# An expert-mixing and convolution kernel: the first matmuls, the first stage of the token transform, and the planner's price of a 16-bit transfer are changed

## The chip, the cores and the metric

The kernel runs on one core of one Trainium2 chip. The metric is the device time of one execution in microseconds (us). The kernel before took 1466.44 us, the median of three runs (1465.94, 1466.44 and 1466.64).

## What is computed

The input `x` has 2048 tokens of width 576. Two branches are computed from it and mixed by a gate for each token:

```python
g = _sigmoid((x * gate_w).sum(-1, keepdims=True))
a = _A_ref(x, ...)          # long convolution of each channel, plus x * Dskip
b = _B_ref(x, ...)          # 32 heads, each picks 2 of 4096 experts
return g * a + (1 - g) * b
```

Branch A builds a convolution kernel of 2048 taps for each of the 576 channels from 128 complex exponentials, and convolves through a discrete Fourier transform (`Kf`, `Uf`, `Yf = Uf * Kf`, inverse). Branch B makes queries `q = x w_q`, scores them against two tables of 64 keys, takes the best two of each, and from their sums the best two of the four pairs. Each chosen expert `e` contributes `g * gelu(x . u[e]) * v[e]`.

The kernel computes B densely. It has the score tiles (`x` times the product of `w_q` and the keys, then top two), the activation tiles (`x` times all 4096 rows of `u`), one-hot matrices that spread the gates over the experts, and at the end a product of the weighted activations with all 4096 rows of `v`. Values that need more than 16 bits are split into a high and a low half (`hi`, `lo`), both fp16, and three products are added: hi times hi, hi times lo and lo times hi.

## The kernel before

**The planner.** The Python program decides the order on each engine while it is built. `clock[0]` is the planner's time, and it goes forward with TensorE's (PE's) matmuls. Work beside the main loop is written as generators that `spawn` puts in a heap. A generator that has to wait yields, and `pump` resumes it when the planner believes that its operands are ready. `Engine` (lines 117 to 134) prices VectorE (DVE), ScalarE (ACT) and GpSimd (POOL) work; `dma` (199 to 204) prices a transfer at four bytes an element over 340 GB/s plus 2.2 us. The chip then runs each engine's list in that order; an instruction whose operands are late holds up all behind it on its engine.

**Main loop** (1563 to 1601). It hands PE either a score tile (`s`, a pair of eighth `c` of the heads and token block `t`, 128 in all) or an activation tile (`a`, a triple `c, tb, j`, 128 in all). Both are 14 matmuls with 512 moving columns (`triple`, 850 to 862). A score tile leaves work for DVE (`scores_top`), an activation tile one scaling copy on ACT or DVE and a store (`act_post`). A score tile needs `whl[c]`, which `w_half`, `w_fold` and `w_tail` make from two halves of `w_q`, and a quarter of the tokens, `xb[tb]`. An activation tile needs `uhl[c]` (from `u_build`) and `xb[tb]` (from `x_build`).

**The start.** SyncE issues in order the keys `kt`, the first quarter of the tokens (`xs`, `xr`), both halves of the first `w_q` (1152 KB each), then the first eighth of `u` (1024 KB and twice 128 KB) and the constants `cst`. `x_build(0)` squares the tokens, adds the squares over the partitions with five matmuls against ones, reduces to the largest norm on DVE (`nx`), turns it into a power of two (`root_scale`, four small DVE instructions), and splits. The first matmuls of the main loop are score tiles. Every tile waits for whole operands.

**Slots and banks.** Nine large buffers (`slot`) are shared by what is loaded and what is split. Eight PSUM banks are shared: four (`sc`) for the tiles, four (`kb`) for all else while the taps are made, after that `wb`.

**Branch A.** `k_params`, `k_front` and `k_gen` make the taps on POOL, ACT and DVE; `k_store` writes them to memory in fp16. `u_stage1` (977 to 1025) is the first stage of the tokens' transform: 32 positions, two interleaved generators (`half(0)`, `half(1)`). A position's tokens are loaded twice, into partitions 0 to 63 and 64 to 127; ACT makes `h` of all 128, DVE replaces the upper 64 by the low half, and for each half of the channels PE multiplies `h` by the tables `tu[:, 0]` and `tu[:, 1]` with 128 rows. It uses one bank at a time. When all taps are stored and `u_stage1` has ended, `freq` (1164 to 1200) runs beside the score tiles. It loads the taps again (`ksb`, four transfers of 1152 KB, each held back until the planner sees the wire free), then the tables `tk` (two of 1024 KB), runs `k_stage1`, then `products`, and afterwards opens the buffers for the one-hot matrices (`ab`) and spawns `prep(0)`.

**The end.** After the last tile the program waits until the activations are stored and `ab` exists (line 1602). The last loop (1611 to 1641) multiplies each block's weights, made by `prep`, with `v` (`o`), with the inverse transform (`y`) beside it.

Of the kernel before, what the change touches and what calls it, by code (L numbers as in the profile page):

```python
# [24 lines left out]
D = 576  # L25
# [19 lines left out]
def _tables():  # L45
# [24 lines left out]
    tu = np.ascontiguousarray(stacked(U_PAIRS).reshape(128, 32, 2, 128))  # L70
# [67 lines left out]
def body(ctx: ExitStack, tc: tile.TileContext, xT, au, par, logdt, dskip, gatew, wq, kT, uT, vv,  # L138
# [60 lines left out]
    def dma(o, i, q=None):  # L199
        t = max(clock[0], rdy.get(key(i), 0.0), queue[0])  # L200
        queue[0] = t + 0.45
        wire[0] = max(wire[0], t) + 4 * o.shape[0] * size(o) / 3.4e5
        rdy[key(o)] = max(rdy.get(key(o), 0.0), wire[0] + 2.2)
        (q or DQ).dma_start(o, i)
# [217 lines left out]

    def x_load(tb):
        a = slot([4, 512], F32, f"xs{tb}")
        r = pl.tile([128, 512], F32, tag="xr", name=f"xr{tb}", bufs=2)
        c = slice(512 * tb, 512 * tb + 512)
        dma(a, xT[0:512, c].rearrange("(k p) n -> p k n", p=128))
        dma(r[0:64], xT[512:576, c])
        dma(r[64:128], xT[512:576, c])
        return a, r  # L430
# [14 lines left out]

    def x_build(tb):
        while tb and tb - 1 not in scaled:
            yield 0.3
        if tb:
            yield from need("slot", 2)  # L450
            xl[tb] = x_load(tb)
        a, r = xl.pop(tb)
        while tb and 0 not in uhl:
            yield 0.3
        b = slot([9, 512], F16, f"xb{tb}")
        sq = b[:, 0:5].bitcast(BF16)
        yield from ready(a, r)
        if tb:
            S.activation(sq[:, 0:4, :], a, AF.Square)
        else:  # L460
            S.activation(sq[:, 0:2, :], a[:, 0:2], AF.Square)
            V.tensor_mul(sq[:, 2:4, :], a[:, 2:4], a[:, 2:4])
        S.activation(sq[:, 4, :], r, AF.Square)
        yield from ready(b)
        yield from need("kb")
        p = bank("kb", f"x{tb}")
        for k in range(5):
            mm(p, onesb, sq[:, k, :], k == 0, k == 4)
        yield from ready(p)
        V.tensor_reduce(out=nx[:, tb:tb + 1], in_=p, axis=AX, op=OP.max)  # L470
        free("kb", nx)
        s, i = root_scale(nx[:, tb:tb + 1], 1.02)
        V.tensor_copy(i_x[:, tb:tb + 1], i)
        yield from ready(s)
        for o, i in [(b[:, k], a[:, k, :]) for k in range(4)] + [(b[:, 8], r)]:
            if tb == 0 or S.free > V.free + 2.0:
                V.tensor_scalar(o, i, s, None, op0=OP.mult)
            else:
                S.activation(o, i, AF.Copy, scale=s)
        scaled.append(tb)  # L480
        for k in range(4):
            yield from ready(b)
            V.scalar_tensor_tensor(b[:, 4 + k], a[:, k, :], s, b[:, k], op0=OP.mult, op1=OP.subtract)
# [9 lines left out]
    whl, wl, sk, halves, scaled, squared = {}, {}, [], {}, [], []  # L493
# [23 lines left out]

    def w_half(c, h, w):
        fl = lambda x: x.rearrange("p a b -> p (a b)")
        yield from ready(w)  # L520
        pbs = []
        acc = newcol(True), newcol(True)
# [3 lines left out]
        squared.append(h)  # L526
        if c == 0:
            yield from w_fold(c, h, w, pbs, ("kb", "kb", "kb") if h == 0 else ("kb", "sc", "sc"))
# [3 lines left out]
        tag = side() if c else "sc"  # L532
# [12 lines left out]
        if c:  # L545
            yield from w_fold(c, h, w, pbs, (side(),) * 3)
        for k, tag, pb in pbs:
            spawn(w_tail(c, k, pb, hl, rem, o, count, s, tag), 0.3 * k)
        del pb, pbs
        free("slot")  # L550
        if c > 0:
            free("raw")
        if h == 0 and c > 0:
            spawn(w_next(c, 1))
# [25 lines left out]

    def w_next(c, h):
        while sdone[0] < c - (kdone[0] == NCK) and 8 * NT - len(groups) < NT * c - 5:
            yield 0.3
        yield from need("raw")
        take("raw", "raw")
        yield from need("slot")
# [304 lines left out]
    gated, placed = [], []  # L891
# [85 lines left out]
    def u_stage1():  # L977
# [5 lines left out]
        ended = []  # L983

        def half(m):
            for n in range(m, 2 * NT, 2):
                a, o = us[:, m, :], us[:, 2 + m, :]
                for z in range(2):
                    l, far = U_PAIRS[n]
                    dma(a[64 * z:64 * z + 64], bass.AP(tensor=au.tensor, offset=au.offset + l * D,  # L990
                                                       ap=[[64 * D, R1], [(far - l) * D, 2], [1, D]]))
                tu = uf.tile([128, 2, 128], F16, tag="tu", name=f"tu{n}", bufs=2)
                dma(tu, tu_d[:, n])
                yield from ready(a, tu)
                h = uf.tile([128, D], F16, tag="uh", name=f"uh{n}", bufs=2)
                S.activation(h, a, AF.Copy, scale=s_u)
                yield from ready(h)
                V.scalar_tensor_tensor(h[64:128], a[64:128], s_u[64:128], h[64:128], op0=OP.mult, op1=OP.subtract)
                yield from ready(h)
                for hh in range(2):  # L1000
                    tag = side()
                    yield from need(tag)
                    pb = bank(tag, f"u1_{n}_{hh}")
                    for z in range(2):
                        mm(pb[:, :288], tu[:, z], h[:, 288 * hh:288 * hh + 288], z == 0, z == 1)
# [4 lines left out]
                    del pb  # L1010
                yield from ready(ov)
                dma(pair_rows(su_d, n), o)
            ended.append(m)

        spawn(half(0))
        spawn(half(1), 3)
        while len(ended) < 2:
# [9 lines left out]
    def k_stage1(ksb, fk):  # L1027
# [11 lines left out]
        def load(w0):  # L1039
            tkt = fk.tile([128, 16, 2, 128], F16, tag="tk", name=f"tk{w0}", bufs=2)  # L1040
            dma(tkt, tk_d[:, w0:w0 + 16, :])
            return tkt

        tabs = load(0), load(16)
# [18 lines left out]
    def products(ff):  # L1063
# [21 lines left out]
        def tail(g, pbs, v):  # L1085

            t = ff.tile([128, 2, 2, PW], F32, tag="tt", name=f"tt{g}", bufs=2)
# [76 lines left out]
    def freq():  # L1164
# [4 lines left out]
        ksb = KS.__enter__().tile([128, 4, NCK // 2, 32, 2 * NI], F16, name="ksb")  # L1169
        for j in range(4):  # L1170
# [4 lines left out]
        fk = FK.__enter__()  # L1175
        spawn(v_norm(), 40)
        spawn(gating(0), 20)
        yield from k_stage1(ksb, fk)
# [21 lines left out]
        v_pool(5, 8)  # L1200


    def u_load(c):
# [3 lines left out]
        dma(a, uT[0:512, cs].rearrange("(k p) n -> p k n", p=128))  # L1207
        dma(r[0:64], uT[512:576, cs])
        dma(r[64:128], uT[512:576, cs])
        return a, r  # L1210

    uhl, i_u, uraw = {}, {}, []

    def u_build(c):
        while adone[0] < c - (kdone[0] < NCK or sdone[0] >= 7):
            yield 0.3
        yield from need("raw")
        take("raw", "raw")
        yield from need("slot")
        a, r = u_load(c)  # L1220
        uraw.append(c)
        yield from ready(a, r)
        while len(squared) < 2:
            yield 0.3
# [3 lines left out]
        yield from squares(a, r, sq, nu[:, c:c + 1])  # L1228
        s, i = root_scale(nu[:, c:c + 1], 1.02)
# [4 lines left out]
        rem = wrems[c % 2]  # L1234
        for k in range(4):
            yield from split(hl[:, 0, k, :], hl[:, 1, k, :], a[:, k, :], s)
        S.activation(rem[:, 0, :], r, AF.Copy, scale=s)
        yield from ready(rem)
        V.scalar_tensor_tensor(rem[0:64, 1, :], r[0:64], s[0:64], rem[0:64, 0, :], op0=OP.mult, op1=OP.subtract)
        free("slot", hl)  # L1240
        free("raw", hl)
        uhl[c] = hl, rem
        yield from ready(rem)
        if c < 7:
# [251 lines left out]
    def finish(t, po):  # L1496
# [7 lines left out]
        for d, o in au_rows(out, t, a):  # L1504
# [6 lines left out]
            for j in range(4)]  # L1511
    dma(kt, kT)
    xl = {0: x_load(0)}
    w_load(0, 0)
    w_load(0, 1)
    V.memset(onesb, 1.0)
# [7 lines left out]
    def k_split():  # L1524
# [159 lines left out]
```

## Time and profile before

| What | us |
|---|---|
| median of three runs | 1466.44 |
| the profiled execution | 1466.58 |
| its span, first to last instruction | 1464.7 |
| outside the span | 1.88 |
| last tap matmul (`kb`) starts | 606.5 |
| last product of the inverse (`pv`) starts | 936.4 |
| first matmul of the last loop (`o`) | 1009.14 |

The span is what the profile's rows add up to. A stage's busy share doesn't show how dense PE runs, since a matmul's row is longer than the time until the next can start; the distance of the rows of a run of matmuls shows it.

### The profile page before, as it was taken

Reading aid. Unit: us, or ns where it says so; the run is one execution under the profiler, and the core shown is the slowest. Engines: PE = TensorE matmul, PEld = TensorE weight load, DVE = VectorE, ACT = ScalarE, POOL = GpSimd, SP = SyncE. Lnnn points to the kernel's source line nnn. Section 1 sums busy time; section 2 is a strip of 40 time slices with the busy share of each in tenths; the row PEclk is TensorE's granted clock in tenths of the full one; section 3 lists DMA queues with packets and bytes.
Section 4 is the critical chain, followed back from the end, with each engine's and each line's share of the span. In section 5 each row is a group of like instructions: output and inputs, shape, how many; then the busy total and the mean of one; then the engine's idle time right before and its main releaser. Section 6 shows DMA issues by size and latency. Waiting matters only on the chain.

```text
span 1464.7 us, 36789 instructions
## 1 busy us (share of the span) xinstructions
PE 1431.2 (98%) x14025; PEld 858.4 (59%) x14028; DVE 1248.5 (85%) x4589; ACT 790.6 (54%) x1315; POOL 532.0 (36%) x511
## 2 busy tenths in 40 slices
PE   5999999999999999999999999998999999999999
PEld 2445454554544544555555444455787787788787
DVE  6989989989999699959899898579998998898860
ACT  5647767698697787434656544576424224223310
POOL 0443545556745645201246799622100110110100
PEclk8999999999999999999999999999999999999999
DMA  9235433372434534384768666677533432442400
GB/s 319 81 93 162 128 94 118 111 213 89 147 104 133 160 107 135 109 263 138 254 211 290 232 200 206 221 239 221 157 111 116 133 125 85 138 147 68 156 10 17
DMA packets 139185, 221.21 MB, mean 151 GB/s; under 512 B 11648, under 2 KB 82688, under 8 KB 132608
## 3 DMA queue, kind: packets, MB, share of 16 engines
q1 hardware_dynamic: 138912, 218.78, 46.5%
q8 instruction: 110, 1.80, 0.5%
q14 instruction: 67, 0.55, 0.1%
q10 hardware_dynamic: 96, 0.07, 0.0%
HBM read 147.51 MB, written 71.30 MB: 149 GB/s over the span
## 4 chain that ended last, share of the span: by engine, by line
PE 84%; DVE 10%; DMA 3%; ACT 1%; issue 1%; SPq 1%; POOL 1%; DVEq 0%; ACTq 0%; POOLq 0%
PE o L213 24%; PE a L213 23%; PE s L213 22%; PE S L213 4%; PE wb L213 2%; PE kb L213 2%; DVE i L133 2%; PE pr L213 2%; DVE m L133 1%; PE u L213 1%; PE y L213 1%; PE kP L213 1%; DVE e L133 1%; PE pv L213 1%; DVE uh L133 1%
## 5 line engine op out<-in xcount | busy, mean ns | idle before, releaser
L213 PE MATMUL o<-vhl,wh 128*128 128x288 f16 x3072 | 387.0, 286 | 0.0
L213 PE MATMUL s<-whl,xb 128*128 128x512 f16 x1536 | 369.5, 382 | 5.0 <-DVE whl L133 4.2
L213 PE MATMUL a<-xb,uhl 128*128 128x512 f16 x1536 | 361.1, 379 | 0.4 <-DVE ko L133 0.4
L213 PEld LDWEIGHTS <-wh 128*128 128x128 f16 x3072 | 296.0, 98 | 76.3 <-issue 3.7
L213 PEld LDWEIGHTS <-xb 128*128 128x128 f16 x1792 | 171.8, 98 | 213.1 <-issue 27.1
L213 PEld LDWEIGHTS <-uhl 128*128 128x128 f16 x1536 | 148.2, 98 | 175.7 <-issue 2.8
L133 DVE FIND_INDEX8 i<-m,s 128x8 uint32<-128x64 f32 x1024 | 206.5, 222 | 0.0
L133 ACT ACTIVATE wh<-gl,s_wg 128x1024 f16<-128x1024 f32 x64 | 68.9, 1137 | 200.3 <-DVE gl L133 200.3
L133 DVE MAX8 m<-s 128x8 f32<-128x64 f32 x1024 | 146.4, 215 | 28.1 <-PE s L213 27.8
L133 POOL TENSOR_TENSOR CS<-CS,ex 128x512 f32<-128x512 f32 x72 | 100.2, 1423 | 139.0 <-DVE ex L133 120.0
L133 POOL TENSOR_TENSOR ya<-ya,db 128x576 f32<-128x576 f32 x16 | 32.0, 2012 | 305.2 <-DMA ya<-in_au_dram 143.6
L133 ACT ACTIVATE go<-a,i_a 128x512 f32<-128x512 f32 x95 | 64.2, 686 | 82.5 <-PE a L213 54.7
L133 POOL TENSOR_TENSOR e<-aN,rt 128x512 f32<-128x512 f32 x72 | 87.5, 1234 | 50.9 <-PE kb L213 47.6
L133 DVE SCALAR_TENSOR_TENSOR wh<-gl,s_wg,wh 128x1024 f16<-128x1024 f32 x64 | 92.4, 1474 | 11.3 <-ACT wh L133 11.3
L133 DVE TENSOR_TENSOR gl<-S,gl 128x256 f32<-128x256 f32 x256 | 90.0, 415 | 7.3 <-PE S L213 7.3
L133 DVE TENSOR_TENSOR Bg<-Be,vals 128x1024 f16<-128x1024 f16 x128 | 90.6, 749 | 2.2
L133 ACT ACTIVATE gl<-gl 128x1024 f32<-128x1024 f32 x64 | 63.5, 1045 | 34.8 <-DMA gl<-g_d 34.8
L133 DVE TENSOR_TENSOR A<-iota_a,vals 128x2048 f16<-128x2048 f16 x64 | 80.5, 1258 | 0.0
L213 PE MATMUL S<-Bg,A 128*128 128x64 f16 x2048 | 73.0, 193 | 5.1 <-DVE Bg L133 4.2
L213 PEld LDWEIGHTS <-A 128*128 128x128 f16 x2048 | 70.6, 97 | 11.2 <-DVE Bg L133 4.1
L213 PE MATMUL s<-wrem,xb 128*128 128x512 f16 x256 | 76.2, 379 | 0.0
L213 PE MATMUL a<-xb,wrem 128*128 128x512 f16 x256 | 76.2, 379 | 0.0
(203 smaller groups left out, 2205.7 us busy)
## 6 DMA issues: line engine op xcount, KB each, us to landing
g_d<-go SPq DMA_DIRECT2D x128, 256.0 KB, 2.7
gl<-g_d SPq DMA_DIRECT2D x32, 1024.0 KB, 5.4
wq<-in_wq_dram SPq DMA_DIRECT2D x16, 1152.0 KB, 6.3
us<-in_au_dram SPq DMA_DIRECT2D x64, 144.0 KB, 3.0
su_d<-us SPq DMA_DIRECT2D x32, 288.0 KB, 2.6
sk_d<-k1o SPq DMA_DIRECT2D x32, 288.0 KB, 2.8
vn<-in_vv_dram SPq DMA_DIRECT2D x32, 288.0 KB, 3.7
ui<-su_d SPq DMA_DIRECT2D x16, 576.0 KB, 4.0
```

The costliest lines, as they stand in the source:

```text
L133: return f(*a, **k)
L213: T.matmul(o, l, r, start=start, stop=stop)
```

## The change

It has six parts.

1. **The first tiles are the activations of the first token quarter.** SyncE now issues the tokens, then `u`, then `kt`, the second token quarter, the two halves of `w_q` and `cst`; the first two operands come in halves (`halves_load`). The scales come from the sum of all squares (ACT's accumulators and three one-column matmuls) and not from the largest norm. PE runs eight matmuls against ones whose results are overwritten (`x_norm(0)`), and then the four activation tiles of `(0, 0)` side by side in four banks, piece by piece as the split pieces come: first all products with the high half of `u`, then those with its low half. The squares of `w_q`, its folding and the largest norm of the first quarter wait until the second quarter is scaled (`1 in scaled`); the third quarter waits for `whl[0]`, the second eighth of `u` for all four quarters.
2. **`u_stage1` takes two positions at a time**, one on partitions 0 to 63 and one on 64 to 127; DVE makes the low half of both at once in a second buffer; PE runs three products for each in pairs of 64 rows, into four banks that are taken together.
3. **`dma` prices fp16 and bf16 elements at two bytes.**
4. **`tk` is loaded ahead of `ksb`.**
5. `products` has three buffers `tt` in place of two.
6. `w_next` starts the next load when 2 tiles of the eighth are left in place of 5, `u_build` gives way to a second half of `w_q` (`second`), and the wait after the last tile is for `shut` in place of `ab`.

```diff
-    tu = np.ascontiguousarray(stacked(U_PAIRS).reshape(128, 32, 2, 128))
+    tu = stacked(U_PAIRS)[0].reshape(R2, 16, 2, 2, 128).transpose(2, 0, 1, 3, 4)
+    tu = np.ascontiguousarray(tu.reshape(128, 16, 2, 128))
...
-        wire[0] = max(wire[0], t) + 4 * o.shape[0] * size(o) / 3.4e5
+        wire[0] = max(wire[0], t) + (2 if o.dtype in (F16, BF16) else 4) * o.shape[0] * size(o) / 3.4e5
...
+    def halves_load(a, src, c):
+        columns.add(a.tensor.name)
+        for m in (0, 2):
+            dma(a[:, m:m + 2], src[128 * m:128 * m + 256, c].rearrange("(k p) n -> p k n", p=128))
...
+    def x_norm(tb, sq):
+        yield from need("kb")
+        p = bank("kb", f"x{tb}")
+        if tb == 0:
+            for k in range(8):
+                mm(p, onesb, sq[:, k % 4, :], True, True)
+            while not marks["s"]:
+                yield 0.1
+        for k in range(5):
+            mm(p, onesb, sq[:, k, :], k == 0, k == 4)
+        normed.append(tb)
+        yield from ready(p)
+        while tb == 0 and 1 not in scaled:
+            yield 0.3
+        V.tensor_reduce(out=nx[:, tb:tb + 1], in_=p, axis=AX, op=OP.max)
+        free("kb", nx)
+    def x_first():
...
+        s, i = yield from scale_first(a, r, sq)
+        spawn(x_norm(0, sq))
+        V.tensor_copy(i_x[:, 0:1], i)
+        for k in range(5):
+            while k == 2 and not marks["s"]:
+                yield 0.1
...
+            V.tensor_scalar(o, src, s, None, op0=OP.mult)
+            V.scalar_tensor_tensor(lo, src[p], s[p], o[p], op0=OP.mult, op1=OP.subtract)
+            marks["x"].append(V.free + 0.28)
...
+        for n, m in enumerate((0, 2)):
+            yield from ready(a[:, m:m + 2])
+            S.activation(sq[:, m:m + 2], a[:, m:m + 2], AF.Square, accum_out=sc[:, acc[n + 1]])
...
-        while sdone[0] < c - (kdone[0] == NCK) and 8 * NT - len(groups) < NT * c - 5:
+        while sdone[0] < c - (kdone[0] == NCK) and 8 * NT - len(groups) < NT * c - 2:
...
+        for p in range(NT):
+            a, tu = ld.pop(p)
+            yield from ready(a, tu)
+            while ended[0] < p - 1:
+                yield 0.3
+            h = uf.tile([128, 2, D], F16, tag="uh", name=f"uh{p}", bufs=2)
+            S.activation(h[:, 0], a, AF.Copy, scale=s_u)
+            yield from ready(h)
+            V.scalar_tensor_tensor(h[:, 1], a, s_u, h[:, 0], op0=OP.mult, op1=OP.subtract)
+            if p + 1 < NT:
+                load(p + 1)
...
+            tag = side()
+            yield from need(tag, 4)
+            pbs = [[bank(tag, f"u1_{p}_{g}_{hh}") for g in range(2)] for hh in range(2)]
+            for hh in range(2):
+                cs = slice(288 * hh, 288 * hh + 288)
+                for n, (z, w) in enumerate(((0, 0), (0, 1), (1, 0))):
+                    for g in range(2):
+                        r = slice(64 * g, 64 * g + 64)
+                        mm(pbs[hh][g][:, :288], tu[r, z], h[r, w, cs], n == 0, n == 2, 0.063)
...
+        tabs = [fk.tile([128, 16, 2, 128], F16, tag="tk", name=f"tk{w0}", bufs=2) for w0 in (0, 16)]
+        for w0, tkt in zip((0, 16), tabs):
+            dma(tkt, tk_d[:, w0:w0 + 16, :])
         for j in range(4):
             while wire[0] > clock[0] + 2:
                 yield 0.3
             dma(ksb[:, j].rearrange("p c w i -> p c (w i)"),
...
+    for w, n in ((0, 9), (1, 5)):
+        for xk in [x for k in range(4) for x in (k, 4 + k)[:2 - w]] + [8]:
+            k = 4 if xk == 8 else xk % 4
+            landed("x", k)
+            landed("hu"[w], k)
+            for j in range(4):
+                cs = slice(128 * j, 128 * j + 128)
+                mm(first[j], wrems[0][:, w, cs] if k == 4 else first_u[0][:, w, k, cs], first_u[1][:, xk, :],
+                   w == 0 and xk == 0, w == 1 and k == 4)
+            pump()
...
-    until(lambda: min(stored) == 32 and ab)
+    until(lambda: min(stored) == 32 and shut)
```

260 lines of the change are left out of this document (170 added, 90 removed).

## The prediction

> **What bounds the kernel now.** I read the page first, then busy time by stage, then the chain of waits, then the start in order of time.
>
> ```profile
> span 1464.7 us, 36789 instructions
> PE 1431.2 (98%) x14025; PEld 858.4 (59%) x14028; DVE 1248.5 (85%) x4589; ACT 790.6 (54%) x1315; POOL 532.0 (36%) x511
> ```
>
> PE is busy for 98% of the span. A busy share says little of how dense PE is, so I take the chain's runs of one kind of matmul (start, length, count):
>
> ```profile
> 359.62 15.11 PE a L213 x70
> ...
> 1408.19 52.93 PE o L213 x432
> ```
>
> A matmul with 512 columns takes 15.11/70 = 0.216 us, one with 288 columns 52.93/432 = 0.1225 us. The stages (window; length, then busy us and count of PE, PEld, DVE, ACT, POOL; clock granted; DMA) show where PE falls short:
>
> ```profile
> 0.00:26.00 26.00, 9.20 (x156) 6.66 (x157) 16.79 (x51) 18.05 (x33) 0.20 (x4) 0.89 0.94 333
> 26.00:31.00 5.00, 4.66 (x13) 1.72 (x13) 2.92 (x5) 2.97 (x4) 0.00 (x0) 0.57 0.86 313
> 31.00:100.00 69.00, 68.84 (x321) 31.29 (x322) 66.85 (x350) 35.39 (x55) 28.42 (x19) 1.00 0.31 94
> 100.00:560.00 460.00, 457.18 (x4355) 232.02 (x4354) 413.68 (x1433) 348.12 (x517) 252.96 (x199) 1.00 0.43 130
> ...
> 1005.00:1041.00 36.00, 30.86 (x356) 23.94 (x355) 35.83 (x50) 16.30 (x20) 11.34 (x7) 1.00 0.64 201
> 1041.00:1465.00 424.00, 419.61 (x4800) 338.78 (x4798) 340.98 (x545) 121.17 (x122) 24.61 (x12) 1.00 0.32 104
> ```
>
> From 31 us to the end PE is filled, except at the seam from 1005 to 1041 us, where 5.1 us are free and DVE has none. So the time is PE's work plus its gaps, and the one large gap is the first 31 us, where the DMA share is 0.94: the data are what PE waits for, then DVE and ACT. In order of time (start, us, engine, what, idle before):
>
> ```profile
> 6.84 1.06 ACT L133 ACTIVATE xb<-xs 128x1024 bf16<-128x1024 f32 x1 [3.75 <-DMA xs<-in_xT_dram]
> 7.95 2.29 PE L213 MATMUL x<-xb,onesb 128*128 128x512 bf16 x5 [4.54 <-ACT xb L133]
> ...
> 10.79 1.16 ACT L133 ACTIVATE wj<-wq 128x1152 bf16<-128x1152 f32 x1 [2.37 <-DMA wq<-in_wq_dram]
> ...
> 14.35 2.32 PE L213 MATMUL wb<-kt,wq 128*64 128x64 f32 x72
> ...
> 20.84 0.16 PE L213 MATMUL sq<-sc,onesb 128*128 128x2 bf16 x1 [4.04 <-ACT uhl L133]
> 21.55 0.59 PE L213 MATMUL s<-whl,xb 128*128 128x512 f16 x1 [0.55 <-ACT whl L133]
> ...
> 26.34 4.50 PE L213 MATMUL s<-whl,xb 128*128 128x512 f16 x11 [4.20 <-DVE whl L133]
> ```
>
> The tokens are there at 6.84 us, but the first dense run starts at 26.34, and its eleven matmuls take 4.50 us, 0.41 each, because the granted clock is 0.57 in that window.
>
> **Part 1, the start.** Up to 30.6 us the kernel before has done the two foldings of `w_q` (2 x 2.32 = 4.6 us) and 12 score matmuls (2.6 us at the full rate): 7.2 us of work that counts. Then it runs dense. What the new start can do comes from these rows:
>
> ```profile
> 11.01 0.15 DVE L133 TENSOR_SCALAR sc<-nx 128x1 f32<-128x1 f32 x1
> ...
> 11.71 1.67 DVE L133 TENSOR_SCALAR xb<-xs,sci 128x512 f16<-128x512 f32 x4
> ...
> 13.65 1.16 ACT L133 ACTIVATE wj<-wq 128x1152 bf16<-128x1152 f32 x1 [0.31 <-DMA wq<-in_wq_dram]
> ...
> 15.23 0.74 DVE L133 SCALAR_TENSOR_TENSOR xb<-xs,sci,xb 128x512 f16<-128x512 f32 x1
> ...
> 18.17 1.91 ACT L133 ACTIVATE uhl<-us 128x2048 bf16<-128x2048 f32 x1
> ...
> 23.47 2.56 ACT L133 ACTIVATE uhl<-us,sci 128x512 f16<-128x512 f32 x4
> ```
>
> - Arrivals. Keys, tokens and one `w_q` half, 64 + 1280 + 1152 = 2496 KB, were there at 10.79 us; with the second half, 3648 KB, at 13.65. New order: tokens 1280 KB, about 7.2 us; `u`, 2560 KB, 10.9 us; second quarter, 3904 KB, 14.3 us.
> - Token scale: squares of the last half 1.06, its sum and a small matmul 0.4, `root_scale` 0.70 (11.01 to 11.71): 9.4 us. A piece then costs DVE 0.42 + 0.74 = 1.16; two are ready by 11.7.
> - Scale of `u`: the same 2.2 us after 10.9 is 13.1. ACT makes a high piece in 0.64, so the first stands at 13.8. The five norm matmuls that count (2.29 at the low clock) stand ahead: I take 14.4 us for the first activation matmul.
> - From there PE is the slow one: 56 matmuls (9 + 5 pieces, 4 tiles) at 0.216 are 12.1 us. DVE has the tokens at 13.1 + 3 x 1.16 = 16.6 and the low pieces of `u` at 16.6 + 5 x 0.74 = 20.3. With the second quarter's five norm matmuls (1.1) PE ends at 27.6.
> - The second quarter: ACT is done with `u` at 16.4, with its squares (1.91 + 0.6) at 18.9; DVE reduces and scales after 20.3 (1.4) to 21.7; ACT splits by 25.0, DVE by 25.7. That is 1.9 us before PE wants it.
>
> So by 30.6 us PE has done 12.1 + 1.1 + 3.0 = 16.2 us of work in place of 7.2: **-9.0 us**. Ends: -10 if the clock is granted early and norm matmuls take 1.1; -6 if it comes a window late (half rate over 3.4 us loses 1.7) and the second quarter 1.3 late. The eight matmuls that are thrown away lie in the wait for `u` (9.4 to 12.8 at 0.43); they cost nothing while `u` needs until 12.
>
> **Part 2, the first stage of the transform.**
>
> ```profile
> L133 DVE SCALAR_TENSOR_TENSOR uh<-us,sci,uh 64x576 f16<-64x576 f32 x32 | 44.5, 1397 | 1.4 <-ACT uh L133 0.6
> ...
> L133 ACT ACTIVATE us<-u 128x288 f32<-128x288 f32 x64 | 24.7, 406 | 15.9 <-PE u L213 15.7
> L133 ACT ACTIVATE uh<-us,sci 128x576 f16<-128x576 f32 x32 | 24.5, 769 | 6.2 <-DMA us<-in_au_dram 6.1
> ```
>
> Sixteen DVE instructions of 1.4 us and sixteen of ACT of 0.77 go (22 and 12 us), but from 100 to 560 us PE is full, and this shortens only the queues behind it. What counts is PE: 128 matmuls of 0.1225 (15.7 us) go; 192 with 64 rows come. Do two of them run side by side? Rows of 64x64 matmuls, and of a change of tiling:
>
> ```profile
> 752.97 0.43 PE L213 MATMUL pr<-ui,cst 64*64 64x256 f32 x2
> 752.98 0.43 PE L213 MATMUL pi<-ui,cst 64*64 64x256 f32 x2
> 753.24 0.38 PE L213 MATMUL pr<-ui,cst 64*64 64x256 f32 x2
> ...
> 943.84 2.75 PE L213 MATMUL a<-xb,uhl 128*128 128x512 f16 x12
> 946.52 0.31 PE L213 MATMUL tr<-identb,vals 128*64 128x64 bf16 x4
> ```
>
> Four records of 256 columns start within 0.27 us; one after another at the pace of the 512-column tiles they would need 0.43. So 64-row groups overlap, and I take 96 pairs at 0.126 = 12.1 us. A change of tiling shows as a gap: twelve matmuls from 943.84 are through at 946.43, the next kind starts at 946.52. That is 0.09 us, and 16 steps have 32 changes: 2.9 us. Sum 12.1 + 2.9 - 15.7 = **-0.7 us**. Ends: -3.6 without gaps, +10.7 if pairs run in turn (192 x 0.1225 + 2.9 - 15.7).
>
> The Trainium skill, TensorEngine Tiling (Array Packing), section Key Properties, says that a change of the tiling mode drains TensorE. It speaks against this part, and the 0.09 us gap agrees with it; without that rule the part would give -3.6.
>
> **Parts 3 and 4, pricing and `tk`.**
>
> ```profile
> L204 SPq DMA_DIRECT2D ksb<-k_d x4: 675/694/773, 612.6 to 640.2; - x4
> ...
> DMA to landing us min/median/max: 6.7/6.8/6.9
> ...
> 640.88 5.33 SPq L204 DMA_DIRECT2D tk<-in_tk_dram x2
> ...
> 662.88 0.65 PE L213 MATMUL k<-ksb,tk 128*128 128x288 f16 x4
> ```
>
> The planner spaced the four `ksb` by 6.9 us each, plus what lay between; each landed 6.8 us after its issue, about 4.6 of it transfer. At two bytes it prices 3.5, and 3.1 for a `tk`. From 612.6: 6.2 + 13.9 + 2.2 + some 7 for stores and a `w_q` between is about 642, not 662.88. PE has score tiles meanwhile, so this gains PE nothing there; but four transfers priced 1.1 us short may make it wait: 0 to 4.4 us. The stores and `w_q` between are priced at four bytes and leave slack, so I take **+1**.
>
> The seam gains from a branch that ends up to 21 us earlier:
>
> ```profile
> 1007.61 0.20 PE L213 MATMUL S<-Bg,A 128*128 128x64 f16 x1 [2.26 <-DVE Bg L133]
> ```
>
> `prep` needs the one-hot matrices from DVE, full from 1005 on. PE comes 9 us earlier, the score tiles end earlier too, and the branch comes 21 earlier, so DVE can start earlier by more than PE. I take **-2**, between -5.1 (the whole gap) and +9 (DVE stays where it was).
>
> **Parts 5 and 6.** The largest wait in the products is `pi` for the DVE reading score tiles in a bank, not for `tt`:
>
> ```profile
> 888.88 0.43 PE L213 MATMUL pi<-ui,cst 64*64 64x256 f32 x2 [1.67 <-DVE m L133]
> ```
>
> So `tt` gives nothing, with ends of -1.7 and +1.7. Later loads of `w_q` are covered by activation tiles; the wait for `shut` ends before `prep` has made the weights that the next loop needs anyway. I cost both at nothing; if that cover fails, PE waits for a `w_q` load, at most the 10.79 us in which the first one came.
>
> **Sum.** -9.0 - 0.7 + 1 - 2 = -10.7 us on the profiled execution's 1466.58 (span 1464.7 and 1.9 around it): 1455.9. The median of the runs is 0.14 lower, so **1455.8 us**.
>
> **Rivals.**
>
> *The start is half given back* (chance 0.16). The activation tiles of two quarters are used up by about 44 us, and then only score tiles are left until the third quarter is split. They cost DVE
>
> ```profile
> 36.39 1.14 DVE L133 MAX8 m<-s 128x8 f32<-128x64 f32 x8
> ...
> 39.04 1.14 DVE L133 MAX8 m<-s 128x8 f32<-128x64 f32 x8
> ```
>
> 2.65 us each against 3.02 on PE, and DVE was busy 66.85 of 69 us up to 100. A quarter costs DVE 1.4 + 5 x 0.74 = 5.1 us more, for which PE has no cover: +5, 1461 us. Against it: banks let PE run some tiles ahead.
>
> *The pairs don't overlap* (0.06): +10.7 in place of -0.7, 1467 us, no change.
>
> *The taps come late* (0.08), the case on the other side. A transform step now takes all four `kb` banks, and only when all are free. It holds them for twelve matmuls and four copies of 0.406, at least 2.4 us, in which the tap generator gets none: 16 x 2.4 = 39 us, and more while a step waits, since the frequency branch also waits for the last step. The branch has gained 21 us by parts 3 and 4. If the taps end later by more than that, PE runs out of tiles and the end follows the branch: each further us is one on top of the time before. With 39 us that is +18, 1484 us; with 30, 1475. Against it: DVE and ACT get 34 us back in the same stretch.
>
> *More of the gaps close* (0.12): the whole seam (-5.1), no wait at `ksb`, the 1.7 us above: 1450 us.
>
> **Chances.** Forecast 0.58, with a range of its own of 1451 to 1460. Within 0.2% (2.9 us, about what a measurement can tell) lie the pairs that don't overlap and the edge of the first rival; faster 0.84, same 0.08, slower 0.08. The range from 1449 to 1464.5 leaves out the late taps, the pairs and a little at each end.
>
> **What would show it.** Right: activation matmuls from 14 to 15 us on, 0.216 apart, and a second run of them before 30; pairs of `u` 0.126 us apart; `k` matmuls from about 642 us; the first `o` near 999 us. Wrong: gaps in PE between 30 and 60 us with DVE full; `u` matmuls 0.12 us apart each; a last `kb` after 630; PE idle ahead of the first `o` by more than 5 us.

## The result and the profile after

The changed kernel takes 1459.87 us (median of six runs, 1458.99 to 1460.11) against 1466.54 for the kernel before, run beside it (1465.36 to 1467.70): ratio 0.9949 with a 95% interval of 0.9939 to 0.9959, or -6.7 us. The forecast was 1455.8 and its range 1449 to 1464.5. The profiled execution has a span 7.5 us shorter than before:

```profile
span 1457.2 us, 36809 instructions
...
PE 1430.8 (98%) x14103; PEld 853.1 (59%) x14105; DVE 1221.5 (84%) x4576; ACT 770.8 (53%) x1294; POOL 519.8 (36%) x512
```

PE's share says as little as before. The start of the changed kernel in order of time (start, us, engine, what, idle before) shows where the time came from:

```profile
9.49 3.57 PE L214 MATMUL x<-xb,onesb 128*128 128x512 bf16 x8
...
11.61 1.06 ACT L134 ACTIVATE uhl<-us 128x1024 bf16<-128x1024 f32 x1 [0.25 <-DMA us<-in_uT_dram]
...
12.86 0.27 PE L214 MATMUL sq<-sc,onesb 128*128 128x1 bf16 x3
...
12.98 2.27 PE L214 MATMUL x<-xb,onesb 128*128 128x512 bf16 x5
...
13.84 2.56 ACT L134 ACTIVATE uhl<-us,sci 128x512 f16<-128x512 f32 x4 [1.07 <-DVE sci L134]
...
15.07 2.77 PE L214 MATMUL a<-xb,uhl 128*128 128x512 f16 x12
...
20.32 1.24 PE L214 MATMUL x<-xb,onesb 128*128 128x512 bf16 x5
...
24.95 2.32 PE L214 MATMUL wb<-kt,wq 128*64 128x64 f32 x72
...
27.20 2.76 PE L214 MATMUL a<-xb,uhl 128*128 128x512 f16 x12
```

The eight matmuls that are thrown away stand first, then the norm matmuls that count, and from 15.07 us activation matmuls 0.22 us apart (from 15.07 to the next kind at 17.68 for twelve). Before, the first dense run stood at 26.34.

The stages of the changed kernel (window; length, then busy us and count of PE, PEld, DVE, ACT, POOL; clock granted; DMA):

```profile
0.00:31.00 31.00, 21.72 (x155) 10.61 (x156) 18.64 (x50) 21.06 (x35) 0.20 (x4) 1.00 0.94 333
...
668.00:940.00 272.00, 265.46 (x2410) 134.17 (x2408) 225.35 (x1422) 151.60 (x422) 177.65 (x240) 1.00 0.70 235
940.00:1100.00 160.00, 157.15 (x1619) 107.84 (x1618) 150.05 (x225) 81.00 (x102) 26.63 (x18) 0.99 0.58 184
```

The same windows of the kernel before:

```profile
668.00:940.00 272.00, 268.37 (x2388) 134.39 (x2386) 235.72 (x1559) 149.25 (x407) 174.02 (x236) 0.99 0.65 220
940.00:1100.00 160.00, 154.34 (x1662) 106.19 (x1661) 145.32 (x232) 84.21 (x118) 30.22 (x20) 1.00 0.61 192
```

PE is free for 2.8 us less in the seam (2.85 of 160 in place of 5.66) and for 2.9 us more in the stretch of the products. The largest waits of PE in the changed kernel after the start are these (engine, line, what it waited for: us in total, times, longest):

```profile
PE pi L214 <- DVE i L134: 3.2, 2, 1.7
PE S L214 <- DVE Bg L134: 2.9, 4, 1.6
...
PE u L214 <- DVE uh L134: 1.8, 2, 1.4
```

The first stage of the transform ends last before the frequency branch now. Rows by tile (count, shortest, median and longest ns, first and last start):

```profile
L214 PE MATMUL u<-uh,tu x192: 279/283/294, 97.1 to 616.0; 64*128 64x288 f16 x192
...
L214 PE MATMUL kb<-e,CS x1152: 219/219/219, 165.0 to 603.6; 128*32 128x64 f32 x192
...
L214 PE MATMUL k<-ksb,tk x128: 285/286/286, 668.7 to 741.7; 128*128 128x288 f16 x128
...
L205 SPq DMA_DIRECT2D ksb<-k_d x4: 670/3307/8617, 624.5 to 639.7; - x4
...
DMA to landing us min/median/max: 11.4/13.9/16.4
```

The last tap is as early as before (603.6 against 606.5), but `u` ends 12 us behind it, so `ksb` is issued from 624.5 on. A `ksb` now lands 13.9 us after its issue and not 6.8. The first `k` stands at 668.7, where 642 was forecast, and the first `o` at 1001.6, where 999 was.

**One number to compare all kernels by.** A gap doesn't tell whether PE catches up later, so I use a lead. Each matmul that counts is priced at the distance that its kind keeps where PE is dense (0.216 us with 512 columns, 0.1225 with 288, small ones likewise; the thrown-away ones at nothing, the transform's first stage at 15.7 us in every kernel). The prices of all that have started by a time are summed, and the sum of the kernel before by the same time is taken off. The last column is the start of the last matmul against that of before. Each row is one profiled execution; beside it the kernel's median and the starts of four matmuls. An execution can lie off its kernel's median: null1's profiled one took 1476.2 us against 1470.3, null2's 1495.0 against 1489.7, bnull2's 1477.4 against 1474.2. Traces lack a few records (the changed kernel's has 26 of the 28 `x` matmuls), so a lead holds to about 0.7 us.

| kernel | median | 31 us | 100 | 560 | 668 | 940 | 1100 | end | last u | last kb | first k | last pv |
|---|---|---|---|---|---|---|---|---|---|---|---|---|
| before | 1466.5 | 0 | 0 | 0 | 0 | 0 | 0 | 0 | 559 | 607 | 663 | 936 |
| changed | 1459.9 | 7.8 | 6.0 | 8.5 | 8.7 | 5.6 | 7.6 | 8.4 | 616 | 604 | 669 | 921 |
| start_only | 1463.1 | 7.6 | 5.6 | 4.1 | 0.9 | 3.9 | 3.8 | 3.8 | 490 | 604 | 657 | 920 |
| no_start | 1512.8 | -0.4 | 0.2 | 1.4 | 1.8 | 7.7 | -46.1 | -46.0 | 684 | 596 | 723 | 973 |
| no_u | 1480.3 | 7.8 | 5.2 | -11.3 | -15.8 | -16.0 | -14.9 | -14.3 | 521 | 638 | 680 | 937 |
| u_two | 1470.2 | 7.5 | 5.6 | -2.8 | -3.1 | -6.0 | -4.3 | -3.6 | 632 | 618 | 687 | 949 |
| u_flow | 1469.5 | 8.0 | 6.7 | 0.8 | -3.0 | -3.3 | -3.2 | -2.5 | 389 | 611 | 642 | 911 |
| u_turn | 1459.9 | 6.9 | 5.2 | 7.2 | 7.4 | 3.6 | 5.3 | 6.0 | 617 | 605 | 670 | 923 |
| price_tk | 1471.6 | -0.6 | -1.5 | -3.4 | -4.0 | -10.4 | -5.9 | -5.8 | 541 | 627 | 661 | 918 |
| no_dummy | 1462.2 | 7.3 | 5.2 | 6.1 | 6.3 | 3.1 | 2.2 | 2.8 | 619 | 606 | 671 | 924 |
| null1 | 1470.3 | 6.4 | 5.0 | 7.2 | 7.4 | -3.3 | -10.4 | -9.7 | 617 | 605 | 671 | 939 |
| null2 | 1489.7 | 7.8 | 6.5 | 4.3 | 3.4 | -4.9 | -29.1 | -28.4 | 659 | 632 | 701 | 962 |
| bnull1 | 1485.0 | -0.2 | -1.5 | -19.9 | -19.6 | -17.6 | -16.2 | -16.8 | 530 | 603 | 668 | 940 |
| bnull2 | 1474.2 | 0.4 | 1.3 | 1.5 | -0.1 | -10.4 | -10.0 | -10.9 | 571 | 617 | 669 | 939 |

### The profile page after: what moved, and what is told of

It is laid out like the page before. It is cut to its first block, busy times and chain, and to the rows that moved or that the text cites. A ratio compares the mean times of both kernels' runs of the same rounds, so it can differ in the third digit from the quotient of the medians.

```text
span 1457.2 us, 36809 instructions
## 1 busy us (share of the span) xinstructions
PE 1430.8 (98%) x14103; PEld 853.1 (59%) x14105; DVE 1221.5 (84%) x4576; ACT 770.8 (53%) x1294; POOL 519.8 (36%) x512
## 4 chain that ended last, share of the span: by engine, by line
PE 83%; DVE 6%; DMA 3%; ACT 1%; issue 0%; SPq 0%; DVEq 0%; ACTq 0%
PE o L214 24%; PE a L214 23%; PE s L214 21%; PE S L214 4%; PE kb L214 2%; PE wb L214 2%; PE pr L214 2%; DVE i L134 1%; PE kP L214 1%; PE y L214 1%; DMA sk_d<-k1o 1%; DVE vhl L134 1%; PE u L214 1%; PE pv L214 1%; PE k L214 1%; DVE m L134 1%
## 5 line engine op out<-in xcount | busy, mean ns | idle before, releaser
L214 PE MATMUL s<-whl,xb 128*128 128x512 f16 x1536 | 364.4, 379 | 0.0
L134 POOL TENSOR_TENSOR CS<-CS,ex 128x512 f32<-128x512 f32 x72 | 95.7, 1361 | 140.0 <-DVE ex L134 138.6
L134 ACT ACTIVATE go<-a,i_a 128x512 f32<-128x512 f32 x85 | 57.5, 683 | 84.4 <-PE a L214 67.1
L134 POOL TENSOR_TENSOR e<-aN,rt 128x512 f32<-128x512 f32 x72 | 83.0, 1173 | 50.4 <-PE kb L214 44.3
L134 DVE SCALAR_TENSOR_TENSOR wh<-gl,s_wg,wh 128x1024 f16<-128x1024 f32 x64 | 87.9, 1406 | 11.3 <-ACT wh L134 11.3
L134 DVE MATCH_VALUE_LOAD i<-m,s 128x8 f32 x1024 | 75.9, 74 | 0.1
```

Source lines behind the costliest of these rows:

```text
L134: return f(*a, **k)
L214: T.matmul(o, l, r, start=start, stop=stop)
```

## The experiments

**start_only and no_start: the start alone, and all but the start.** The first is the changed kernel with the old transform stage, price, place of `tk`, two `tt`, the old `w_next` and no `second`; the second the kernel before with all of these new, and the new wait for `shut`. The core of the first (no_start has such lines the other way, in the kernel before):

```diff
-        wire[0] = max(wire[0], t) + (2 if o.dtype in (F16, BF16) else 4) * o.shape[0] * size(o) / 3.4e5
+        wire[0] = max(wire[0], t) + 4 * o.shape[0] * size(o) / 3.4e5
...
-            yield from need(tag, 4)
...
+                    yield from need(tag)
```

> The new start alone: the first stage of the transform takes one position at a time again, transfers are priced at four bytes, tk is loaded after ksb, two buffers tt, w_q loads and the priority of its second half as before. Theory A (the start is nearly all of the gain): the changed kernel was 7.8 us of priced PE work ahead at 31 us and kept 5 to 8.5 of them, so 5 to 8 us less than before, 1458.5 to 1461.5. Theory B (the start's lead is mostly given back by 130 us and the other parts earn it again): 2 to 5 us less than before, 1461.5 to 1464.5.

> The kernel before with everything but the new start: two positions a step, two-byte prices, tk first, three buffers tt, loads of w_q at 2 tiles (the priority of its second half is left out, as it belongs to the new start's order of u). Theory A: within 2.5 us of before, 1464 to 1469. Theory B: 2 to 5 us less than before, 1461.5 to 1464.5. In both, the span from the last kb matmul to the first k matmul shows the price and the order of tk if the transform's first stage ends first.

Measured: start_only 1463.13 us, ratio 0.9969 (0.9956 to 0.9982); no_start 1512.8, ratio 1.0302 (1.0286 to 1.0318). The start has its 7.6 us by itself and none is there without it; by the end, half of it is left. Its time lies in the range of theory B and not in that of A. The other parts alone cost 46 us, which neither theory had. They were 7.7 us ahead at 940 us and lost everything in the seam:

```profile
PE S L214 <- DVE Bg L134: 31.5, 17, 5.1
```

That is the row of PE's waits in no_start: 17 waits for the one-hot matrices. In the window there PE is busy for 63 of 100 us and DVE for 96, and the clock falls too:

```profile
1000.00:1100.00 100.00, 63.23 (x696) 47.73 (x693) 96.30 (x139) 50.01 (x62) 22.43 (x13) 0.71 0.45 153
```

The reason lies 300 us earlier. The last `u` stands at 684, 88 us behind the last `kb`, so the branch ends at 973, and DVE can begin the one-hot matrices only then.

**null1 and null2: the changed kernel with another number in its planner.** No work is added or removed.

```diff
-        rdy[key(o)] = max(rdy.get(key(o), 0.0), wire[0] + 2.2)
+        rdy[key(o)] = max(rdy.get(key(o), 0.0), wire[0] + 2.25)
```
```diff
-        t = 0.085 + 0.00083 * size(out)
+        t = 0.087 + 0.00083 * size(out)
```

> The changed kernel with one constant of the planner moved by next to nothing: the 2.2 us that a transfer is given to land become 2.25. Nothing that is computed and no order that was meant changes; every later order may. If the plan's luck matters (theory C: the 4.4 us that PE lost between 742 and 900 us are waits in orders that happened to come out badly), the time moves by 1 to 3 us either way and the two pi waits of 1.7 us appear elsewhere or not at all. If the loss belongs to a part of the change (theory D), it stays within 0.7 us of the changed kernel, and PE's lead over before falls by 3 to 5 us in the products again.

> The changed kernel with the planner's fixed price of an ACT instruction moved from 0.085 to 0.087 us. As for the other one: theory C, 1 to 3 us either way from the changed kernel and other waits in the products; theory D, within 0.7 us, with the same loss in the products.

Measured: 1470.26 us, ratio 1.0017 (1.0008 to 1.0027), and 1489.67, ratio 1.0137 (1.0114 to 1.0159): 10 and 30 us over the changed kernel, both over the kernel before. Theory C had 1 to 3 us, so that its idea holds and its size doesn't; theory D falls. In null1's trace, some 94% of PE's matmul records stand in the order of the changed kernel's. It keeps its lead up to 668 us; the products then take 10.7 us of it and the seam 7.1 (in an execution 5.9 us above the median, so part of this may be that execution's own). Its waits:

```profile
PE S L214 <- DVE Bg L134: 7.4, 7, 2.7
PE pi L214 <- DVE m L134: 3.7, 1, 3.7
...
PE pv L214 <- DVE i L134: 2.4, 1, 2.4
```

In null2 the taps and `u` come late (632 and 659), the branch ends at 962, and the seam takes 24 us.

**bnull1 and bnull2: the same two numbers in the kernel before.** The diffs are those of null1 and null2.

> The kernel before with one constant of its planner changed: a transfer is taken to land 2.25 us after its last byte in place of 2.2 (as null1 did to the changed kernel, +10 us there). No work is added or removed. Theory L (the plan's order is fragile in both kernels, and each of them as shown is a lucky one): 1472 to 1500 us, 6 to 33 us over the kernel before, with waits of PE at places where the kernel before has none. Theory F (only the changed kernel's plan is fragile): within 3 us of the kernel before, 1464 to 1470.

> The kernel before with another constant of its planner changed: the fixed price of an ACT instruction 0.087 us in place of 0.085 (as null2 did to the changed kernel, +30 us there). No work is added or removed. Theory L: 1472 to 1500 us. Theory F: within 3 us of the kernel before, 1464 to 1470. If both this one and bnull1 come out over 1472, the mean of the changed kernel's two (1480) against the mean of these two says what the change is worth over plans: theory S (the start's 7.5 us are what the change brings in any plan) expects the means to differ by 3 to 12 us in the changed kernel's favour; with two plans each and a spread of 10 us this can only hint.

Measured: 1484.97 us, ratio 1.0117 (1.0092 to 1.0141), and 1474.23, ratio 1.0048 (1.0031 to 1.0065): +17.5 and +6.8 us on the 1467.48 beside them. Theory L holds: both plans are fragile, and both kernels as shown have better ones than with either number moved. bnull1 lost 18 us between 100 and 560 us, where PE waits for the DVE in several places; the largest:

```profile
PE kP L213 <- DVE nu L133: 3.9, 1, 3.9
```

The two means, 1480.0 us for the changed kernel's and 1479.6 for those of before, don't differ. Theory S expected 3 to 12 us; with a spread of 10 us and two plans each, that neither shows a gain nor excludes one.

**no_u: the old stage of one position in the changed kernel.**

```diff
-            yield from need(tag, 4)
-            pbs = [[bank(tag, f"u1_{p}_{g}_{hh}") for g in range(2)] for hh in range(2)]
...
+                    yield from need(tag)
+                    pb = bank(tag, f"u1_{n}_{hh}")
```

> The changed kernel with the old first stage of the transform (one position at a time, one bank at a time); all else as changed. Theory E (a step that wants four banks at once ends late, and the frequency branch waits for it: in the changed kernel the last u stands at 616.0, 12 us behind the last kb at 603.6): here the last u stands before the last kb, the first ksb is issued at 604 to 612 right behind the last tap store, k begins at 635 to 650, products end before 915, and the time is 1452 to 1459 us, under the changed kernel. Theory L (the time follows from how the whole planned order happens to fall out, and the transform's step is one disturbance among many): the last u may well be early, but the time lies anywhere from 1450 to 1490 and doesn't go with the start of the branch. Theory P (the pairs save what the prediction said, 0.7 us, and nothing hangs on the banks): 1460 to 1461.5 us.

Measured: 1480.28 us, ratio 1.0081 (1.0061 to 1.0101). The last `u` came early, at 521, but the last tap stands at 638, and the time is 20 us longer: E and P fall, and L has its case. One wait explains more than half of it. PE in order of time:

```profile
210.10 2.10 PE L213 MATMUL s<-whl,xb 128*128 128x512 f16 x9
223.53 0.64 PE L213 MATMUL u<-uh,tu 128*128 128x288 f16 x2 [11.32 <-DVE uh L133]
223.96 1.49 PE L213 MATMUL s<-whl,xb 128*128 128x512 f16 x3
```

ACT in the same stretch of no_u:

```profile
211.49 0.76 ACT L133 ACTIVATE uh<-us,sci 128x576 f16<-128x576 f32 x1
...
213.18 1.28 ACT L133 ACT_TABLE_LOAD   x1
214.47 1.06 ACT L133 ACTIVATE e<-e 128x1024 f32<-128x1024 f32 x1
...
217.53 1.28 ACT L133 ACT_TABLE_LOAD   x1
...
221.87 1.04 ACT L133 ACTIVATE CS<-CS 128x1024 f32<-128x1024 f32 x1
222.81 0.76 ACT L133 ACTIVATE uh<-us,sci 128x576 f16<-128x576 f32 x1
```

A bundle for the taps (exponentials, sines and two table loads, 213.18 to 222.81) stands in ACT's list ahead of a `uh`, while PE's list has the two `u` matmuls that need it ahead of score tiles whose data are there. Each engine runs its list in order, so a bundle one place too early stops PE for 11.3 us.

**u_two and u_flow: what makes the last u late.** u_two asks for two banks at a time; u_flow also drops the wait for the step before and the planner's 12 us.

```diff
-            yield from need(tag, 4)
-            pbs = [[bank(tag, f"u1_{p}_{g}_{hh}") for g in range(2)] for hh in range(2)]
...
+                yield from need(tag, 2)
+                pbs = [bank(tag, f"u1_{p}_{g}_{hh}") for g in range(2)]
```
```diff
-            while ended[0] < p:
-                yield 0.3
...
-            yield 12
```

> The changed kernel, but a step of the transform asks for two banks at a time, for one half of the channels, and gives them back before it asks for the next two (positions still in pairs of 64 rows; twice as many changes of tiling, 32 more at about 0.1 us each). Theory E: two banks come free sooner than four, the last u stands before the last kb (before 604), k begins near 640 and the time is 1452 to 1459 us in spite of the 3 us of changes. Theory L: the last u is early too, but the time lies anywhere from 1450 to 1490. If four banks are not what makes the step late (the loads or DVE are), the last u stands at 610 or later as in the changed kernel, and the time is at 1460 or over.

> Like u_two (two banks at a time), but a step no longer waits until the copies of the step before it have ended, nor the planner's 12 us: two steps may be in flight, as two positions were in the kernel before. Theory C (the steps follow one another as one chain, 33 us each in the changed kernel and 36 in u_two, against 28 for two positions in two chains before; that is what makes the last u late): 24 to 30 us a step, the last u at 480 to 570, well before the last kb, and the first ksb within 8 us of the last tap store. If banks are what it waits for, the step stays over 32 us and the last u stands after 600. The time of the whole is not foretold by either, since any new order moves it by ten microseconds or more: 1450 to 1490.

Measured: u_two 1470.18 us, ratio 1.0015 (1.0001 to 1.0028), a step every 35.6 us on average and the last `u` at 632: the four banks are not what delays it, and theory E falls. u_flow 1469.51 us, ratio 1.0012 (0.9997 to 1.0026), a step every 18.7 us:

```profile
L214 PE MATMUL u<-uh,tu x192: 279/283/294, 96.7 to 389.0; 64*128 64x288 f16 x192
...
L214 PE MATMUL k<-ksb,tk x128: 285/286/286, 642.0 to 713.7; 128*128 128x288 f16 x128
...
L205 SPq DMA_DIRECT2D ksb<-k_d x4: 956/4221/5413, 616.3 to 627.6; - x4
```

These are its rows by tile. Theory C holds in kind, and its ranges (24 to 30 us, last `u` from 480 on) are left on the far side: without the wait for the step before and the 12 us, a step takes 18.7 us, where the chain of loads, ACT, DVE, banks and copies takes 34.6 in the changed kernel (97.1 to 616.0 for sixteen) and 14.3 for one position, 28.6 for two, in the two interleaved chains before. Both went at once, so which of the two counts is open. With the chain cut, the first `ksb` follows the last tap's store (612.2) by 4 us, `k` begins at 642.0 and the products end at 911, ten microseconds before the changed kernel's. It gains nothing for the end: the lead was lost between 100 and 668 us, and the seam gives none back.

**u_turn: do the pairs overlap because of their order?** Planner and lists are kept, but within a step the three products of the lower rows precede those of the upper.

```diff
-                for n, (z, w) in enumerate(((0, 0), (0, 1), (1, 0))):
-                    for g in range(2):
+                for g in range(2):
+                    for n, (z, w) in enumerate(((0, 0), (0, 1), (1, 0))):
...
+                rdy[key(pbs[hh][0])] = clock[0] - 0.063 + 0.4
```

The last line keeps the planner's times as they were.

> The changed kernel with the order of all engines kept, but inside a step of the transform the three products of the lower 64 rows come first and then those of the upper 64, so that two matmuls in a row use the same rows. If pairs overlap because they use different rows, this costs a step 6 x 0.12 = 0.7 us and all sixteen 11.8 us of PE's work: twelve u matmuls then take 1.5 us in place of 0.84. As PE is filled from 31 to 1000 us, the time should be 1459.9 + 11.8 = 1471 to 1473 us; if the plan has slack that swallows part of it, less, and if later work keeps falling behind its plan, more. If the order within a step makes no difference, 1459 to 1461.

Measured: 1459.91 us, ratio 0.9944 (0.9922 to 0.9967), the same as the changed kernel. Its step, in order of time:

```profile
160.87 0.92 PE L214 MATMUL u<-uh,tu 64*128 64x288 f16 x12
161.72 0.61 PE L214 MATMUL a<-xb,wrem 128*128 128x512 f16 x2
```

and the changed kernel's:

```profile
159.80 0.91 PE L214 MATMUL u<-uh,tu 64*128 64x288 f16 x12
160.64 0.60 PE L214 MATMUL a<-xb,wrem 128*128 128x512 f16 x2
```

Twelve take 0.84 to 0.85 us either way, the change of tiling behind them included; in turn they would take 12 x 0.1225 = 1.47. The pairs overlap, and don't need to stand in pairs. The run says nothing on what 11.8 us more of PE work would do, since there were none. Here an equal plan gave an equal median. Single executions of one plan differ by more: null1's twelve lie between 1467.3 and 1476.2 us.

**price_tk: parts 3 and 4 in the kernel before.**

```diff
-        wire[0] = max(wire[0], t) + 4 * o.shape[0] * size(o) / 3.4e5
+        wire[0] = max(wire[0], t) + (2 if o.dtype in (F16, BF16) else 4) * o.shape[0] * size(o) / 3.4e5
...
+        for w0, tkt in zip((0, 16), tabs):
+            dma(tkt, tk_d[:, w0:w0 + 16, :])
```

> The kernel before with parts 3 and 4 alone: the planner prices 16-bit transfers at two bytes, and tk is loaded ahead of ksb. As the prediction reckoned: k begins at about 642 us in place of 662.9, products end near 915 in place of 936, the seam at 1000 to 1050 loses less and the time is 1462 to 1467 us (+1 and -2 on 1466.5). If the two-byte price makes the planner issue loads and the work behind them too early, k waits for ksb, gaps stand before k, and the time is 1468 to 1475. Theory L: k begins near 642, and the time is off by more than 5 us in either direction without any wait at ksb.

Measured: 1471.63 us, ratio 1.0027 (1.0013 to 1.0041). From the last tap to the first `k` it takes 34.8 us (626.5 to 661.3), as the prediction reckoned (606.5 to 642), and 56.4 before. But the price changes the plan: the taps end 20 us later, and the end is 4 us later, so that none of the three expectations is met as a whole. PE's waits are not at `ksb`:

```profile
PE s L213 <- DVE whl L133: 4.7, 1, 4.7
...
PE pi L213 <- DVE m L133: 3.6, 1, 3.6
```

The first stands at 27 us, in the start, where the kernel before has it too (4.20 us, ahead of 26.34). The second is in the products, which take 6.4 us of the lead (-4.0 at 668, -10.4 at 940); with the branch 18 us earlier than before, the seam then gives 4.5 back (-5.9 at 1100).

**no_dummy: without the eight matmuls against ones.**

```diff
-            for k in range(8):
-                mm(p, onesb, sq[:, k % 4, :], True, True)
```

> The changed kernel without the eight matmuls against ones whose results are overwritten (nothing else left out). If they are there for the granted clock: the clock is under full for part of 14 to 20 us, the first activation matmuls start 0.43 apart in place of 0.22 for up to one window of about 3.4 us, and the first activation run ends 1 to 2 us later. If the five norm matmuls and the small ones do as well, the clock rows of the start stay as in the changed kernel, and the first activation matmul stands up to 1 us earlier. The time of the whole is read for the start alone, since two changes of a planner's constant by 2% already moved it by 10 and by 30 us.

Measured: 1462.2 us, ratio 0.9964 (0.9951 to 0.9977), with PE's other matmuls in the same order. Its start in order of time:

```profile
13.65 0.16 PE L214 MATMUL sq<-sc,onesb 128*128 128x1 bf16 x1 [1.23 <-ACT uhl L134]
13.67 2.30 PE L214 MATMUL x<-xb,onesb 128*128 128x512 bf16 x5
15.76 3.20 PE L214 MATMUL a<-xb,uhl 128*128 128x512 f16 x12
```

The first twelve activation matmuls take 3.20 us; in each of the eight profiled starts that have the eight matmuls (the changed kernel's, start_only's, no_u's, u_two's, u_flow's, u_turn's and the nulls') they take 2.75 to 2.77. So the eight are worth 0.45 us there; the first of the twelve stood between 14.5 and 16.4 in those runs, as the loads came, a spread wider than that gain. The half rate was there, 0.43 us apart from 13.67 to 16.61, but the five norm matmuls take most of it. Why the whole takes 2.3 us more than the changed kernel isn't shown.

No run had part 5, `w_next`, `second` or `shut` alone; what they are worth is open. None of the versions was faster than the changed kernel.

## Why the prediction was right

The sign and the range were right, and 6.7 us came for a forecast of 10.7. By its terms:

- **The start, -9.0 forecast: -7.8 measured**, in the nine profiles with the new start 6.4 to 8.0, in the four others without it -0.6 to 0.4. The step that was mis-sized is the first activation matmul, put at 14.4 and found at 15.07: the five norm matmuls start at 12.98, behind the eight that are thrown away and the small ones, and run at half rate. The prediction's own figures say so: its eight end at 12.8, and 2.29 us behind that is 15.1. `u` came later as well: ACT could square its last part at 11.61, where 10.9 was reckoned, and had the first high piece at about 14.5 in place of 13.8, still ahead of PE. The late first matmul is 0.7 of the 1.2 us; the rest is not traced to one step. Activation matmuls 0.22 us apart and a second run of them at 17.73 came as foretold.
- **The rival of a start half given back from 31 to 60 us** didn't come: the lead is 7.9 at 60. A window shows DVE busy there for 22 of 29 us:

```profile
31.00:60.00 29.00, 28.87 (x196) 14.18 (x198) 21.98 (x92) 14.61 (x24) 12.35 (x9) 1.00 0.41 121
```

  What was lost, 1.8 us, went between 80 and 100, where PE waits for ACT's squares of the second eighth of `u` and for the first `uh`.
- **The transform's step, -0.7: -0.7.** Twelve matmuls take 0.84 us with the change of tiling behind them (160.64 less 159.80) and 0.09 to 0.10 ahead of them, 0.94 in all; sixteen steps 15.0 us, in place of the 15.7 of before. The drain that the Trainium skill names in TensorEngine Tiling (Array Packing), section Key Properties, is seen on both sides of a step. The `u` matmuls of 128 rows in the kernel before have no such gap (0.216 us from the tile ahead, 0.122 to the one behind). Pairs that run in turn are refuted by the rows, 0.84 us for twelve.
- **The price, +1: not found as such.** PE waits for `ksb` in none of changed, price_tk and u_flow; in null2 it waits 2.6 us. Issued behind the two of `tk`, the four do take longer, 11.4 to 16.4 us from issue to landing in place of 6.8, but the tiles cover it. `k` from 642 failed here: I let the branch follow the last tap and didn't ask when the last `u` comes. In price_tk and u_flow, where `u` is early, the 35.5 us from tap to `k` are there (34.8 and 31.5).
- **The seam, -2: -2.0** (a lead of 5.6 at 940 and 7.6 at 1100), with the branch 15 us earlier (921 against 936), not 21. price_tk, with a branch at 918, gains 4.5 there, but u_flow, with one at 911, gains nothing, so that an earlier branch is worth 2 us isn't shown.
- **The late branch, the case on the other side.** It was rightly seen as the danger and wrongly explained. The taps don't starve (last `kb` 604; in no_start 596); the step itself is late, as a chain. The point from which it decides shows over the runs: where the products' last matmul starts by 949 us, the lead changes from 940 to 1100 by -7.1 to +4.5 us; at 962 it falls by 24 and at 973 by 54. I gave each us that the branch ends later than before one us of time; no_start's ends 37 us later and pays 54, since PE then waits for DVE at each block and the clock is granted at 0.71.
- **Parts 5 and 6, nothing; more gaps close.** The products took 3.1 us of the lead (8.7 at 668, 5.6 at 940), in waits of `pi` for DVE's index search in score tiles. The kernel before had such a wait too (1.67 us), which speaks for the plan and not for `tt`; no run shows it.

The terms that were foretold come to -7.8, -0.7 and -2.0, 10.5 us, almost the forecast's sum. What it had no term for, by the table: 1.8 us lost from 31 to 100, 2.0 won from 100 to 668 beside the step's 0.7, 3.1 lost to 940, 0.8 won after 1100, and 0.9 lost behind the last matmul (4.8 us from its start to the end of the span in place of 3.9). That leaves the profile's 7.5. I put the five that have no term down to the plan, though no run shows that one by one, and that they came to only 3 us is luck. With a number of the planner moved by 2% the time moved by 10 and 30 us in the changed kernel, and by 7 and 18 in the kernel before. So the start's lead, 6.4 to 8.0 us, is shown as far as 31 us, in each of nine profiles; that the change is worth 6.7 us is true of these two plans, and the experiments don't show it for others.

## What to carry to other kernels

Where a program writes out each engine's order ahead of time, a change has two effects: its own work, and a new order, and the second can be several times the first; run both kernels with a harmless number moved before a gain of half a per cent is put down to an edit, and judge by medians of several executions. To judge a part by itself, keep the lists and change only what stands in them (as u_turn did), and read the stage where it acts, not the end. A branch that runs beside a full engine costs nothing up to a point and more than its delay beyond it: look for what it must be ready for, and give it room there first.

## What the runs showed of the hardware

- **Matmuls on other rows overtake.** In u_turn three matmuls on rows 0 to 63 precede three on rows 64 to 127 in the program, yet the records start in pairs: 10 ns apart, the next pair some 112 ns later, six pairs in 13 of the 16 steps. The second record carries the wait that the program as built has at its fourth matmul. The Trainium skill says in TensorE: Matmul & The Clock Gate, Part 3, that matmuls start and end in program order; here the starts don't, across row groups (the profile models the ends).
- **The clock row at the start doesn't tell.** The eight matmuls of 512 columns take 12.86 - 9.49 = 3.37 us, 0.42 each, and the five behind them 2.09, so half rate, while the window's granted clock is 1.00 from 10 to 14 us:

```profile
10.00:14.00 4.00, 4.00 (x14) 1.46 (x13) 3.40 (x14) 2.49 (x6) 0.00 (x0) 1.00 1.06 378
```

  The start of a trace is better read by the distance of equal matmuls.
- **A long wait costs twice.** After the 11.3 us wait in no_u the score matmuls from 223.96 start 0.427 us apart in place of 0.216, and do so until 226.6: PE runs at half rate for some 3 us more.
